# Attention backward: half of the second set of exponentials (queries on the partitions) taken by DMA transposes of the stored score tiles, the other half still recomputed

## The chip, the cores and the metric

One core of one Trainium2 chip. Times are device microseconds of one execution. Every kernel was run several times beside runs of the kernel before on the same chip. Ratios are the mean time of one kernel's fast runs over that of the other's in the same rounds, so they are not quite the ratio of the medians that are quoted beside them.

## The reference

A gated sum of attention without a mask (32 heads of 18, sequence 2048, width 576) and a state-space convolution, with the gradients of all inputs. The change touches only attention, forward and backward. What matters of it:

```python
qkv = (x @ wqkv).reshape(B, S, 3, H, Dh).transpose(2, 0, 3, 1, 4)
scores = jnp.einsum("bhqd,bhkd->bhqk", q, k) * (Dh ** -0.5)
p = softmax(scores, axis=-1)
o = jnp.einsum("bhqk,bhkd->bhqd", p, v)
# the backward pass (jax.vjp) needs, per head:
#   dP = dO V^T,  dS = P * (dP - rowsum(dO * O)),  dQ = dS K,  dK = dS^T Q,  dV = P^T dO
```

## The kernel before

Four heads form a group (8 groups), 512 queries a query block (4 per group). A group and a query block form a unit: 32 units. A unit is walked in 32 half steps, one key tile of 128 for two of the four heads in each; eight half steps are called a round here. In each half step the kernel starts the forward pass of one unit and the backward pass of the unit before it:

- P1: scores with keys on the partitions; their exponentials `PT` are kept (20 tiles of 4 KB per partition).
- P2: `dP` with keys on the partitions; VectorE multiplies it by the kept `PT` and gives `ds`. A DMA transpose makes `dsT` (queries on the partitions) of each finished `ds`.
- P3: the scores again, now with queries on the partitions; their exponentials `eb` feed dV, which contracts over queries.

```python
def row(kind, g, b, l, r, j):                      # one score matmul: 19 rows, one of four row groups
    tg, nb = ("dP", 2) if kind == "P2" else ("S", 4)
    ps = apsp.tile([P, KB], F32, tag=tg, bufs=nb, name="ps_" + kind)
    mm(ps, lhsT=l[r0:r0 + DA], rhs=r[r0:r0 + DA], tile_position=(r0, 0))
...                                                # cut: bursts dv, dq, dk; eight or sixteen matmuls
                                                   # into the one bank accB, then one VectorE addition
for G in range(NTOT + OFF + 16):                   # half steps; the backward pass runs OFF = 37 later
    ...                                            # cut: rows P1 P3 P2 P1 P3 P2
    if G % 4 == 1 and G2 >= 4:  evs.append(dv_burst(...))
    if G % 4 == 2 and G2 >= 5:  evs.append(dq_burst(...))
    if G % 4 in (3, 0) and G2 >= 10: ...           # dK: half a burst, seven and eight half steps
                                                   # after the last ds that it needs
    if G % 4 in (3, 0) and G >= 3: ...             # PV (exponentials times V) of the forward pass, into accO
    for (kind, g, b, i, j, ps) in rows:
        if kind == "P1":
            nc.scalar.activation(U["PT"][i][:, j, :], ps, ACT.Exp)
        elif kind == "P3":
            nc.scalar.activation(e, ps, ACT.Exp)   # e = U["eb"][...]
        else:
            nc.vector.tensor_tensor(U["ds"][i][:, j, :], ps, U["PT"][i][:, j, :], op=A.mult)
            if U["dsn", i] == 4:
                nc.sync.dma_start_transpose(out=U["dsT", p][:, i % 2, :, :], in_=U["ds"][i]...)
```

The kernel shares out eight PSUM banks: four for scores (`S`), two for `dP`, one for `accO`, one for `accB`. All DMAs are issued by SyncE into one queue, in order. The order of TensorE, ScalarE, VectorE and GpSimd is the source's; SyncE's is chosen by the scheduler of the language.

## Time and profile before

| | before |
|---|---|
| median of the first three runs | 4017.24 us (4016.9 to 4019.89) |
| attention, first score matmul to last use of `dsT` | 247.6 to 2587 us |
| both passes running, 290 to 2580 us: PE, ACT, DVE busy | 98%, 91%, 80% |
| DMA share and rate there | 0.79, 139 GB/s |
| one unit, from its first dP matmul to the next unit's: second, third, last, first query block of a group | 70.4, 70.4, 76.8, 71.3 us |

The last row is worked out from the start times of the dP matmuls in the trace. Units of the second and third query block are called middle units below; those of the last and first one lie around a change of group, where the gradients of a group are stored and the next group's operands come in. A middle unit of 70.4 us is four rounds of 17.6 us. The lines behind the other rows stand in the prediction.

### The profile page before, as it was taken

Reading aid. Unit: us, or ns where it says so; the run is one execution under the profiler, and the core shown is the slowest. Engines: PE = TensorE matmul, PEld = TensorE weight load, DVE = VectorE, ACT = ScalarE, POOL = GpSimd, SP = SyncE. Lnnn points to the kernel's source line nnn. Section 1 sums busy time; section 2 is a strip of 40 time slices with the busy share of each in tenths; the row PEclk is TensorE's granted clock in tenths of the full one; section 3 lists DMA queues with packets and bytes.
Section 4 is the critical chain, followed back from the end, with each engine's and each line's share of the span. In section 5 each row is a group of like instructions: output and inputs, shape, how many; then the busy total and the mean of one; then the engine's idle time right before and its main releaser. Section 6 shows DMA issues by size and latency. Waiting matters only on the chain. (4 is left out here: it accounts for less than half of the span.)

```text
span 4013.0 us, 64388 instructions
## 1 busy us (share of the span) xinstructions
PE 3139.8 (78%) x24050; PEld 1049.1 (26%) x24050; DVE 2959.3 (74%) x5147; ACT 2878.7 (72%) x5308; POOL 63.0 (2%) x141
## 2 busy tenths in 40 slices
PE   7979999999999999999999999779244445454411
PEld 2312222222222222222222222136133333333310
DVE  5518877878878878878878878712388888888877
ACT  4459999989989999989989989501366666666401
POOL 0000000000000000000000000100000000000000
PEclk9955555555555555555555555589555555555555
DMA  8436797886787887787887787876455565555447
GB/s 195 164 92 127 129 157 131 134 160 126 132 157 128 134 158 128 135 154 130 138 155 128 133 146 126 175 205 164 83 106 103 104 112 109 106 108 103 71 143 174
DMA packets 1858939, 538.18 MB, mean 134 GB/s; under 512 B 1771743, under 2 KB 1837353, under 8 KB 1858626
## 3 DMA queue, kind: packets, MB, share of 16 engines
q1 hardware_dynamic: 1858626, 534.07, 69.9%
q8 instruction: 189, 3.10, 0.3%
q14 instruction: 124, 1.02, 0.1%
HBM read 102.10 MB, written 60.96 MB: 41 GB/s over the span
## 5 line engine op out<-in xcount | busy, mean ns | idle before, releaser
L601 DVE TENSOR_TENSOR ds<-ps_P,PT 128x512 bf16<-128x512 f32 x2048 | 1360.8, 687 | 369.8 <-PE ps_P L30 226.0
L592 ACT ACTIVATE PT<-ps_P 128x512 bf16<-128x512 f32 x2048 | 1250.2, 615 | 186.4 <-PE ps_P L30 186.4
L596 ACT ACTIVATE eb<-ps_P 128x512 bf16<-128x512 f32 x2048 | 1262.6, 618 | 21.3 <-PE ps_P L30 21.2
L30 PE MATMUL ps_P<-dOaT,VaT_g 19*128 19x512 bf16 x2048 | 1145.0, 601 | 36.1 <-DMA VaT_g<-VaT_d 32.3
L30 PE MATMUL ps_P<-KaT_g,QaT_g 19*128 19x512 bf16 x2048 | 1105.2, 593 | 5.8 <-ACT PT L592 5.8
L30 PE MATMUL ps_P<-QaT_g,KaT_g 19*128 19x512 bf16 x2048 | 1055.0, 613 | 9.9 <-DMA KaT_g<-KaT_d 5.9
L30 PE MATMUL accO<-PT,Vtok_g 128*32 128x512 bf16 x2048 | 331.6, 632 | 0.0
L30 PEld LDWEIGHTS <-KaT_g 19*128 19x128 bf16 x2048 | 135.9, 103 | 740.9 <-issue 721.0
L30 PE MATMUL accK<-dsT,Qtok_g 128*32 128x256 bf16 x4096 | 314.8, 407 | 8.9 <-DMA Qtok_g<-QaT_d 5.7
L30 PEld LDWEIGHTS <-VaT_g 19*128 19x128 bf16 x2048 | 196.3, 98 | 383.5 <-issue 345.4
L30 PE MATMUL accQ<-ds,Ktok_g 128*32 128x512 bf16 x2048 | 266.9, 620 | 1.3 <-DVE dvacc L461 0.8
L30 PE MATMUL accV<-eb,dOa 128*32 128x512 bf16 x2048 | 267.0, 621 | 0.6 <-DVE dkacc L502 0.6
L30 PE MATMUL uvp<-RX,E1e 128*128 128x64 bf16 x1152 | 134.2, 290 | 106.1 <-DVE E1e L892 106.1
L30 PE MATMUL tps<-RX,T0w 128*128 128x32 bf16 x576 | 38.4, 233 | 215.1 <-DVE yd L1027 189.9
L873 ACT ACTIVATE kk<-ph,magc 128x512 f32<-128x512 f32 x144 | 91.1, 686 | 148.1 <-DVE E1e L891 112.7
L30 PE MATMUL ph<-thr,lrow 3*128 3x512 bf16 x288 | 127.5, 576 | 86.1 <-ACT ab L866 59.3
L30 PEld LDWEIGHTS <-QaT_g 19*128 19x128 bf16 x2048 | 158.8, 99 | 128.5 <-issue 123.0
L461 DVE TENSOR_TENSOR dvacc<-dvacc,accV 128x512 f32<-128x512 f32 x224 | 154.1, 688 | 34.4 <-PE accV L30 29.4
L478 DVE TENSOR_TENSOR dqa<-dqa,accQ 128x512 f32<-128x512 f32 x224 | 153.8, 687 | 34.0 <-PE accQ L30 28.5
L30 PEld LDWEIGHTS <-E1e 128*128 128x128 bf16 x1152 | 125.2, 124 | 127.1 <-DVE E1e L892 126.5
L30 PE MATMUL ybp<-Rw,E1n 128*128 128x31 bf16 x1152 | 70.1, 233 | 104.1 <-ACT ydi L964 101.4
L910 ACT ACTIVATE UV<-uvp 128x512 bf16<-128x512 f32 x144 | 86.0, 597 | 85.1 <-PE uvp L30 85.1
(273 smaller groups left out, 3392.2 us busy)
## 6 DMA issues: line engine op xcount, KB each, us to landing
T0w<-Kp_d SPq DMA_DIRECT2D x36, 512.0 KB
dsT<-ds SPq DMA_TRANSPOSE x512
dqkv_d<-dtk SPq DMA_DIRECT2D x96, 72.0 KB
dqkv_tok<-dqkv_d SPq DMA_DIRECT2D x1, 6912.0 KB
Md_d<-mst SPq DMA_DIRECT2D x144, 36.0 KB
ga_d<-ga_st SPq DMA_DIRECT2D x16, 288.0 KB
dxm_d<-dxm SPq DMA_DIRECT2D x16, 288.0 KB
skw<-Md_d SPq DMA_DIRECT2D x72, 64.0 KB
```

The source lines that it names most:

```text
L30: return nc.tensor.matmul(out, lhsT=lhsT, rhs=rhs, start=start, stop=stop, **kw)
L461: nc.vector.tensor_tensor(a_, a_, acc, op=A.add)
L478: nc.vector.tensor_tensor(U["dqa"], U["dqa"], acc, op=A.add)
L592: nc.scalar.activation(U["PT"][i][:, j, :], ps, ACT.Exp)
L596: nc.scalar.activation(e, ps, ACT.Exp)
L601: nc.vector.tensor_tensor(U["ds"][i][:, j, :], ps, U["PT"][i][:, j, :], op=A.mult)
L873: nc.scalar.activation(B_["kk"][h][:, 4 * q:4 * q + 4, :], ph, ACT.Identity, bias=magc, scale=1.0)
L910: nc.scalar.mul(UV[:, ri, :, c0:c0 + 8], pr, -1.0 if ri == 0 else 1.0)
```

## The change

The kernel already holds the exponentials with keys on the partitions. A transpose of such a tile gives what P3 recomputes. The change takes tiles 0 and 1 of every four this way (`PTT`), and recomputes only tiles 2 and 3. It wants to free ScalarE of a quarter of its exponentials and TensorE of a sixth of its score matmuls. To make room it rewrites the schedule of a round, takes one buffer where there were two in many places, and merges the dV part of the transposed tiles into the dK burst. Cut to its core:

```diff
-                OFF = NST + 5
+            OFF = 41
+            PTB = 22
...
+                def turn(R, k):
+                    if k == 0:
+                        U["PTT", r] = work.tile([P, 2, 4 * TPQ, P], BF, tag="PTT", bufs=1, name="PTT")
+                    nc.sync.dma_start_transpose(out=U["PTT", r][:, k, :, :], in_=U["PT"][4 * r + k].rearrange("p j q -> p (j q)"))
+
+                def q_pair(R, n_):                       # P3, for tiles 2 and 3 of four only
+                    ...
+                def dk_burst(R, k):
+                    for w in range(2 if k == 0 else 1):
+                        ...
+                                if w == 0:
+                                    l_, r_ = grp_t[g]["Qtok"][:, b * TPQ + qb, j, :], U["dsT", 2 * r + k]
+                                else:
+                                    l_, r_ = U["dOa"][:, qb, j, :], U["PTT", r]
+                        ...
+                            def fin():
+                                store_grad(a_[:, 0::2, :], g, 1, list(range(4 * r, 4 * r + 4)), 1.0)
+                                store_grad(a_[:, 1:2, :], g, 2, [4 * r, 4 * r + 1], 1.0)
...
+                    half(hs)                             # rows P1 P2 P1 P2
+                    R, c8 = divmod(hs - OFF, 8)
+                    acts = {0: "dqA pv t1", 1: "dv q0", 2: "dk2", 3: "pv", 4: "pv q1", 5: "dk4", 6: "q2 dqB t0", 7: "q3 pv"}[c8].split()
...
-                    gb = work.tile([P, KB], BF, tag="gb", name="gb")
+                    gb = work.tile([P, n, P], BF, tag="gb", bufs=1, name="gb")
```

(`dsT` from 3 buffers to 2; `gb`, `gT`, `dtk`, `dO`, `Ob`, `oT`, `dqa` from 2 to 1; `dvacc` from 4 to 2.) In the table `acts`, dk4 is the long dk burst (its last `ds` is finished in half step 3, two before), dk2 the short one, t0 and t1 ask for the two PTT transposes, a q pair (q0 to q3) is two recomputed score matmuls and their exponentials, dqA and dqB are the two dQ bursts. Half steps of a round are numbered 0 to 7, as in the prediction.

## The prediction

> **What bounds the kernel now.** I read the page first: the busy slices, then the groups. Attention runs from the first score matmul at 247.6 us to the last use of a transposed tile at 2586.9 us (the view of tile `dsT`), so it is 58% of the span, and only it is changed.
>
> ```profile
> PE   7979999999999999999999999779244445454411
> ACT  4459999989989999989989989501366666666401
> PEclk9955555555555555555555555589555555555555
> DMA  8436797886787887787887787876455565555447
> ```
>
> Each digit is a slice of 100 us. In slices 3 to 25 TensorE and ScalarE are both full, TensorE at half clock, and the DMA engines are not far behind. The window table gives the sums for the part with both passes running (columns: length, then busy time of PE, PEld, DVE, ACT, POOL with counts, granted clock, DMA share, GB/s):
>
> ```profile
> 290.00:2580.00 2290.00, 2240.32 (x16312) 522.85 (x16312) 1820.46 (x2997) 2084.74 (x4145) 39.50 (x92) 0.50 0.79 139
> ```
>
> PE 98%, ACT 91%, DVE 80%, DMA 0.79. The list of waits in the attention stretch says which of the two full engines leads:
>
> ```profile
> DVE ds L601 <- PE ps_P L30: 204.8, 356, 2.9
> ACT PT L592 <- PE ps_P L30: 168.2, 412, 5.4
> ...
> PE ps_P L30 <- ACT PT L592: 5.0, 20, 0.3
> ```
>
> ScalarE and VectorE wait for TensorE; TensorE waits 5 us in all for ScalarE. **TensorE's queue is the bound**, with ScalarE just under it. The timeline gives its beat:
>
> ```profile
> 1502.12 0.60 PE L30 MATMUL ps_P<-QaT_g,KaT_g 19*128 19x512 bf16 x1
> ...
> 1502.52 0.63 PE L30 MATMUL ps_P<-QaT_g,KaT_g 19*128 19x512 bf16 x1
> ...
> 1503.10 1.04 PE L30 MATMUL accQ<-ds,Ktok_g 128*32 128x512 bf16 x8
> 1504.08 0.60 PE L30 MATMUL ps_P<-QaT_g,KaT_g 19*128 19x512 bf16 x1
> ```
>
> Score matmuls on different row groups start together, so they go in waves: six per half step in two or three waves, 0.40 us apart, and 0.53 us from the last wave to a burst. A burst of eight 512-column matmuls takes 0.98 us. Half steps alternate between 1.96 us and 2.30 us (1502.12, 1504.08, 1506.38, 1508.34), so eight of them, which I call a round, take 4 x 4.26 = 17.0 us. There are 1024 half steps, 128 rounds, 32 units (a group and a query block) of 4 rounds. 128 x 17.0 = 2181 us; the other 109 us of the 2290 are the fp32 transposes after each forward pass and the stalls where a group changes.
>
> **What the Trainium skill says.** "TensorE: Matmul & The Clock Gate", Part 1, knows two states of the clock, half and full, and gives 426.7 ns start to start for 512 columns at half; the trace agrees (0.50 for the whole stretch, waves 0.39 to 0.45 us apart). It has granted half already with TensorE 98% busy, so I expect no better from a kernel that keeps TensorE less busy. "ScalarE: Activation LUTs", What ACT_TABLE_LOAD costs, gives 186 ns + 0.833 ns per element and an overlap of about 93 ns, that is 613 ns long and 520 ns apart for 512; the trace has 0.60 to 0.62 us and a closer 0.48 us apart. "Advanced Engine Details and Errata", X-Bar Transpose (TRN2), says that transpose DMAs are as fast as regular ones, and "DMA: Bandwidth & Descriptors", Latency and other measured facts, has 261 GB/s for one with a non-contiguous middle dimension. Here both are too high for the transpose in question:
>
> ```profile
> 1563.00:1563.50 0.50, 0.50 (x11) 0.14 (x8) 0.50 (x2) 0.50 (x2) 0.00 (x0) 0.50 0.76 152
> 1563.50:1564.00 0.50, 0.50 (x8) 0.00 (x0) 0.50 (x2) 0.50 (x2) 0.00 (x0) 0.50 1.13 214
> 1564.00:1564.50 0.50, 0.50 (x8) 0.23 (x5) 0.47 (x2) 0.50 (x2) 0.00 (x0) 0.50 1.16 212
> 1564.50:1565.00 0.50, 0.50 (x6) 0.10 (x1) 0.50 (x2) 0.50 (x2) 0.00 (x0) 0.50 1.17 218
> 1565.00:1565.50 0.50, 0.50 (x7) 0.14 (x8) 0.46 (x2) 0.50 (x2) 0.00 (x0) 0.50 1.14 209
> 1565.50:1566.00 0.50, 0.50 (x8) 0.00 (x0) 0.50 (x1) 0.50 (x2) 0.00 (x0) 0.50 0.23 44
> 1566.00:1566.50 0.50, 0.50 (x7) 0.13 (x5) 0.21 (x2) 0.50 (x2) 0.00 (x0) 0.50 0.00 0
> ```
>
> One `dsT` transpose of 512 KB (524,288 bytes) fills all 16 engines for about 2.6 us with ramps, at 209 to 218 GB/s; the straight loads before attention reach over 400 GB/s. Back to back I take 524 KB / 214 = 2.45 us. A share above 1 means that packets overlap: this is the engines' own limit for this form, not a gap to be filled.
>
> **The change on TensorE, ScalarE and VectorE.** Per round: 16 recomputed score matmuls become 8, in four pairs. The four matmuls of a half step now all lie in different row groups, so one wave. My sum, with rows 0.53 (0.40 when score matmuls follow), bursts 0.85 or 0.98 where the mode changes, a PV 0.43 or 0.56, a q pair 0.40, the long dk burst 1.84: 1.94 + 1.94 + 1.51 + 1.09 + 1.52 + 2.37 + 1.91 + 1.49 = **13.8 us**, against 17.0. The columns of the bursts stay equal: half of the dV work only moves from `eb` to `PTT`. ScalarE goes from 32 to 24 exponentials, 15.6 to 11.7 us at 0.487. VectorE keeps 16 products at 0.607 us start to start (9.7), and its additions go from 4 x 0.69 + 2 x 0.41 to 4 x 0.69 + 0.41: about 12.9 us. If these engines were all, a round would take 14 to 14.5 us and attention would fall by about 350 us.
>
> **The change on DMA.** 512 `dsT` transposes stay and 256 `PTT` transposes of the same shape come: 6 per round instead of 4, 6 x 2.45 = **14.7 us**. The window moved 139 GB/s x 2290 us = 318 MB, 268 of it `dsT`; the other 50 MB (loads of a group at 290 to 410 GB/s, gradient transposes at 290, the 72 KB stores and loads in small pieces at about 0.6 us each) need some 240 us, 1.9 us per round. So the DMA needs 128 x (14.7 + 1.9) = 2125 us, and the old stretch was 2290. The spare 20% is spent on this.
>
> **The DMA then has to be fed without a gap, and the schedule does not allow that.** All transposes go through one queue in order, from one sequencer. A transpose starts to move 1.2 us after it is issued. I follow a round from the end of the long dk burst (fifth half step), which frees the only `PTT` buffer: the first PTT transpose moves from 1.2 to 3.65. The next `dsT` needs the products of the seventh half step: rows at 1.9, products done about 4.1, moving from 5.3 (1.65 us idle). From there four transposes run on without a gap (that `dsT`, the second PTT, two more `dsT`): 5.3 + 9.8 = 15.1. The long dk burst needs the last of them: it reads the product tile finished only two half steps earlier (before: six or seven). TensorE reaches it at 12.1 and **stalls 3 us**. It ends at 15.2 + 1.7 = 16.9. So a round is 16.9 us, what it was, before the other transfers. Of their 1.9 us some falls into the 2.2 us of gaps; most comes between the four transposes and adds to the path. I take 1.0 to 1.4: 17.9 to 18.3 us.
>
> **Sum.** 128 x 18.0 = 2304. The forward's transposes, 2 us per unit before, now mostly lie in TensorE's stall. Where a group changes it gets worse: the last unit of a group took 77 us against 70 for the others; `gb`, `gT`, `dtk`, `dO`, `Ob` and `oT` go from two buffers to one, a group's gradient stores go from 12 to 14, and dK and half of dV are stored one right behind the other, so ScalarE waits with the second `gb` until the first was transposed, behind a full queue. I put 7 to 10 us on each of 8 groups, 70. Start: four half steps more without a second pass, 5 us. 2304 + 70 + 5 = 2379 against 2290: +90, so 4017 + 90, about **4110 us**.
>
> **Rivals.** (1) The compute bound holds: if the DMA engines take PTT in their gaps and the sequencer orders issues better than the source (SyncE is not among the hand-scheduled engines), a round needs only 15.5 to 16.5 us: 4017 - 64 to 190, 3830 to 3950. For it: TensorE, ScalarE and VectorE all get room, and DMA is 21% idle. Against: it needs over 95% use of the DMA. (2) A wash: the stall takes exactly the place of the saved waves, as in my bare 16.9 us round, 3990 to 4080. (3) Single buffers and head-of-line blocking: the sequencer already waited 108 + 42 us for ScalarE before it could issue a gradient transpose, with the DMA 20% idle; now such blocking is lost DMA time. At 3 us for each of 112 stores, 4200 to 4300.
>
> **Range and chances.** 1 us per round is 128 us, and my round is no better than that. So 3960 to 4260. Faster by over 2% needs attention under 2260 us, of which some 48 have no second pass, thus 2125 of DMA in 2210, 96%: 0.13. Within 2%: 0.36. Slower by over 2%: 0.51.
>
> **What would show it.** Right: DMA share in attention up from 0.79 to 1.0 or more, about 195 GB/s; TensorE waiting for DMA `dsT` at `accK` for 150 to 400 us in all; ScalarE's busy time down by 630 us, PE's share of the stretch under 90%, ACT's under 75%; clock 0.50; exponentials in `eb` 1024; PTT transposes as long as `dsT`. Wrong: little waiting for `dsT`, or transposes back to back well under 2.45 us (then rival 1); waits mainly of ScalarE for `gT` (rival 3); or a granted clock of 1.0, which I exclude.

## The result, and the profile after

The changed kernel takes **4464.54 us** (median of 4 runs, 4458.43 to 4465.79), before 4017.07 us beside it: ratio 1.111 (95% interval 1.1091 to 1.1129), 447 us slower. The result is correct. The prediction leaned to slower; the loss was five times the 90 us forecast, outside the range.

The page's slices, as before (each digit 1/40 of the span, now 112 us):

```profile
PE   8877768767767866866776776764934544444411
ACT  5366646656656656655655665630126666666601
PEclk9855555555555555555555555556965555555555
DMA  7469989989988998999999988998645555555447
```

No engine is full any more: in most slices with both passes TensorE has fallen to six to eight tenths and ScalarE to five to six, and the DMA engines stand at eight to nine. The window over the stretch with both passes (length, PE, PEld, DVE, ACT, POOL busy, clock, DMA share, GB/s):

```profile
292.00:3027.00 2735.00, 1983.07 (x16320) 525.62 (x16318) 1726.74 (x2869) 1609.29 (x3130) 42.41 (x108) 0.55 0.92 165
```

The stretch grew from 2290 to 2735 us. TensorE is busy 257 us less in it, ScalarE 475 us less; 165 GB/s x 2735 us is 451 MB, 133 MB more than before, as 256 transposes of 524 KB should be. So the work went as intended, and waits more than replaced it. The list of waits from 300 to 3000 us (who waited for whom: total, times, longest):

```profile
ACT PT L493 <- PE ps_P L30: 731.5, 373, 5.8
PE accK L30 <- DMA dsT<-ds: 505.3, 218, 5.9
...
ACT gb L421 <- DMA gT<-gb: 182.3, 46, 8.2
PE ps_P L30 <- ACT PT L493: 173.2, 35, 9.0
...
PE ps_P L30 <- DVE ds L498: 11.3, 24, 1.0
```

ScalarE waits for TensorE, and TensorE for `dsT`. Where, the timeline of TensorE shows (start, length, instruction, idle time ahead of it and who ended it):

```profile
1718.25 0.37 PE L30 MATMUL ps_P<-dOaT,VaT_g 19*128 19x512 bf16 x1
1722.57 1.04 PE L30 MATMUL accK<-dsT,Qtok_g 128*32 128x256 bf16 x16 [3.95 <-DMA dsT<-ds]
...
1727.02 0.63 PE L30 MATMUL ps_P<-dOaT,VaT_g 19*128 19x512 bf16 x2
1729.97 1.05 PE L30 MATMUL accK<-dsT,Qtok_g 128*32 128x256 bf16 x16 [2.32 <-DMA dsT<-ds]
```

It stalls **twice** in a round, at dk2 and at dk4. Over all 128 rounds the idle time ahead of dk2 is 1.78 us in the median, 259 us in all, and ahead of dk4 2.27 us and 269 us (worked out from the trace). The 3.95 us shown at dk2 are therefore not typical: the data of its `dsT` had all moved at 1720.2, but from 1721.0 to 1722.2 the DMA moved next to nothing (5 GB/s, a 16 KB packet of the page's instruction queue starts at 1720.6), and its semaphore was complete only at 1722.5, 2.3 us after the last data; the PTT transpose before it needed 0.5 us for this. The timeline of the issuing sequencer over the same time says why dk2 waits at all:

```profile
1711.37 4.49 SPq L514 DMA_TRANSPOSE PTT<-PT  x2
1715.91 14.95 SPq L504 DMA_TRANSPOSE dsT<-ds  x4
1731.91 4.24 SPq L514 DMA_TRANSPOSE PTT<-PT  x2
```

In the source a `dsT` stands between t0 and t1. In the queue the two PTT transposes are neighbours (in 121 of the 128 rounds), and the `dsT` that dk2 needs lies behind both. At dk4 it is something else: that `dsT` was issued at 1725.53 with the DMA engines idle, and the burst waited for its bare latency, 4.4 us from issue to burst. The sequencer's line, and windows of the DMA (last two columns: share, GB/s):

```profile
1725.53 1.94 SPq L504 DMA_TRANSPOSE dsT<-ds  x1
```

```profile
1723.80:1726.70 2.90, 2.90 (x20) 0.51 (x18) 2.70 (x5) 2.17 (x4) 0.00 (x0) 0.50 0.00 0
1726.70:1729.30 2.60, 0.95 (x6) 0.04 (x6) 1.45 (x3) 2.04 (x4) 0.00 (x0) 0.50 1.05 202
```

For 2.9 us nothing moved: TensorE's stall at dk2 had held back the products, and there was nothing to issue. Then one transpose moved alone while TensorE stood at dk4. In such a round the two take turns: TensorE waits for the DMA, and then the DMA for TensorE.

From the start times of the dP matmuls, as before (median per half step in middle units; the sum of the medians is called an undisturbed round, and it lies below the mean round: 17.3 against 17.6 us before the change, 19.4 against 19.7 after it):

| half step | 0 | 1 | 2 | 3 | 4 | 5 | 6 | 7 | round |
|---|---|---|---|---|---|---|---|---|---|
| predicted TensorE work | 1.94 | 1.94 | 1.51 | 1.09 | 1.52 | 2.37 | 1.91 | 1.49 | 13.8 |
| changed kernel | 2.10 | 1.92 | 3.32 | 1.41 | 2.06 | 4.74 | 1.95 | 1.87 | 19.4 |
| `e1`: PTT without its volume | 2.11 | 1.92 | 2.11 | 1.42 | 2.06 | 4.77 | 1.95 | 1.87 | 18.2 |

Units by query block (second, third, last, first): 77.8, 80.1, 93.1, 92.1 us, against 70.4, 70.4, 76.8, 71.3. If all units had grown by the 8.6 us of the middle ones, 32 x 8.6 = 274 us would be lost; the units around a change of group grew by another 8 to 12 us each, some 160 us over 16 units.

### The profile page after: what moved, and what is told of

Same layout as the page of the kernel before. It is cut to its first block, busy times and chain, and to the rows that moved or that the text cites. A ratio compares the mean times of both kernels' runs of the same rounds, so it can differ in the third digit from the quotient of the medians.

```text
span 4464.0 us, 63571 instructions
## 1 busy us (share of the span) xinstructions
PE 2890.1 (65%) x24050; PEld 1055.1 (24%) x24050; DVE 2865.8 (64%) x5019; ACT 2405.4 (54%) x4300; POOL 65.7 (1%) x157
## 5 line engine op out<-in xcount | busy, mean ns | idle before, releaser
L493 ACT ACTIVATE PT<-ps_P 128x512 bf16<-128x512 f32 x2048 | 1120.3, 612 | 734.0 <-PE ps_P L30 733.1
L30 PE MATMUL ps_P<-dOaT,VaT_g 19*128 19x512 bf16 x2048 | 756.9, 572 | 44.1 <-DMA VaT_g<-VaT_d 30.1
L30 PE MATMUL ps_P<-QaT_g,KaT_g 19*128 19x512 bf16 x2048 | 696.4, 575 | 134.7 <-ACT PT L493 128.6
L535 ACT ACTIVATE eb<-ps_P 128x512 bf16<-128x512 f32 x1024 | 561.3, 610 | 177.2 <-PE ps_P L30 175.8
L30 PE MATMUL ps_P<-KaT_g,QaT_g 19*128 19x512 bf16 x1024 | 351.0, 584 | 49.4 <-ACT PT L493 46.5
L459 DVE TENSOR_TENSOR dkacc<-dkacc,accK 128x512 f32<-128x512 f32 x192 | 106.2, 553 | 413.9 <-PE accK L30 413.9
L30 PEld LDWEIGHTS <-Qtok_g 128*32 128x32 bf16 x4096 | 125.7, 125 | 722.6 <-issue 480.2
L918 DVE SCALAR_TENSOR_TENSOR kk<-kk,ph 128x512 f32<-128x512 f32 x144 | 95.1, 682 | 71.2 <-ACT kk L913 71.2
L30 PEld LDWEIGHTS <-Vtok_g 128*32 128x32 bf16 x2048 | 61.5, 110 | 331.8 <-issue 329.4
L30 PE MATMUL accK<-PTT,dOa 128*32 128x256 bf16 x2048 | 138.7, 420 | 0.0
```

The source lines that it names most:

```text
L30: return nc.tensor.matmul(out, lhsT=lhsT, rhs=rhs, start=start, stop=stop, **kw)
L459: nc.vector.tensor_tensor(a_, a_, acc, op=A.add)
L918: nc.vector.scalar_tensor_tensor(v_, v_, MAGIC, B_["ph"].pop((h, q)), op0=A.subtract, op1=A.subtract)
```

## The experiments

All times are medians of 4 runs, beside runs of the kernel before (4017 to 4026 us). Units are given as second, third, last and first query block.

| run | time, us | ratio to before (95%) | units, us |
|---|---|---|---|
| changed kernel | 4464.5 | 1.111 (1.1091 to 1.1129) | 77.8, 80.1, 93.1, 92.1 |
| e1_small_ptt (wrong) | 4272.9 | 1.062 (1.0600 to 1.0642) | 72.7, 74.1, 86.9, 85.3 |
| e2_late_dk | 4230.7 | 1.051 (1.0495 to 1.0530) | 70.7, 70.2, 87.9, 84.6 |
| e3_two_store_buffers | 4403.8 | 1.095 (1.0925 to 1.0967) | 77.6, 80.2, 92.8, 84.7 |
| e4_before_more_dma | 4138.1 | 1.028 (1.0267 to 1.0298) | 70.4, 72.1, 85.6, 75.7 |
| e5_late_small (wrong) | 4138.0 | 1.029 (1.0269 to 1.0315) | 70.4, 70.4, 82.2, 79.7 |
| e6_late_two_store | 4161.6 | 1.035 (1.0324 to 1.0369) | 69.6, 71.2, 83.7, 79.6 |
| e7_small_two_store (wrong) | 4222.0 | 1.050 (1.0472 to 1.0520) | 73.0, 74.3, 83.8, 81.3 |
| e8_before_one_store | 4043.7 | 1.005 (1.0021 to 1.0081) | 70.4, 70.4, 76.5, 73.6 |
| e9_late_small_dp3 (wrong) | 4173.0 | 1.039 (1.0367 to 1.0404) | 70.8, 70.4, 84.8, 79.9 |
| e10_late_two_store_dp3 | 4152.7 | 1.033 (1.0303 to 1.0354) | 68.9, 69.7, 83.8, 79.3 |
| e11_late_small_accb2 (wrong) | 4211.9 | 1.048 (1.0451 to 1.0501) | 72.0, 71.9, 85.8, 81.5 |
| e12_late_two_store_even | 4158.1 | 1.033 (1.0317 to 1.0348) | 69.2, 70.8, 84.0, 79.9 |
| e13_even_spread_stores | 4154.5 | 1.032 (1.0306 to 1.0340) | 69.4, 70.6, 82.1, 81.3 |
| e14_even_spread_small (wrong) | 3973.9 | 0.989 (0.9868 to 0.9903) | 65.9, 66.9, 74.9, 74.1 |

**Take the volume of PTT away.**

```diff
-                        U["PTT", r] = work.tile([P, 2, 4 * TPQ, P], BF, tag="PTT", bufs=1, name="PTT")
-                    nc.sync.dma_start_transpose(out=U["PTT", r][:, k, :, :], in_=U["PT"][4 * r + k].rearrange("p j q -> p (j q)"))
+                        U["PTT", r] = PTT_all        # zeroed once
+                    nc.sync.dma_start_transpose(out=U["PTT", r][:, k, 0:1, :], in_=U["PT"][4 * r + k][:, 0, 0:P])
```

> The changed kernel, but each PTT transpose carries one 128x128 block of 16 (the rest of PTT stays zero, so a part of dV and its products are wrong on purpose). All instructions, their order and their waits stay; only the DMA time of PTT, 256 x 2.6 us, goes. Theory A (TensorE waits for score-gradient transposes that lie in the queue behind two PTT transposes): the wait of TensorE for dsT at accK falls from 516 us to 50 to 250 us (the dk burst of the fifth half step still follows its product by two half steps), middle units from 78-80 us to 64-70 us, total 3950 to 4130 us. Theory B (the bursts come too soon after their products, however full the queue is): the wait stays over 350 us, total over 4300 us. Theory C (single store buffers): units at the change of a group stay over 90 us, total over 4250 us.

Measured: 4272.9 us, between the theories. In the table of half steps only number 2 moved, from 3.32 to 2.11 us: the stall at dk2 is the queue's doing. Half step 5 stayed at 4.77 us: the stall at dk4 does not come from the volume of PTT. By bursts, the idle time ahead of dk2 fell from 259 to 73 us, ahead of dk4 only from 269 to 264 us. Of the wait for `dsT`, 516 us over the whole trace of the changed kernel, more than half was left (window 292 to 2960 us):

```profile
PE accK L30 <- DMA dsT<-ds: 328.0, 165, 4.4
```

So A and B each hold for one of the two stalls, and more than half of the loss (447 us, of which 192 went here) is not volume. No run put only the order of the queue right, so how much of the stall at dk2 comes from the order, and how much from the volume in whatever order, is not separated.

**Let the bursts run later.** dk4 from half step 5 to the next round's 0, dk2 from 2 to 4, the PTT requests to 1 and 2.

```diff
-  {0: "dqA pv t1", 1: "dv q0", 2: "dk2", 3: "pv", 4: "pv q1", 5: "dk4", 6: "q2 dqB t0", 7: "q3 pv"}
+  {0: "pv dk4", 1: "dv q0 t0", 2: "dqA t1", 3: "pv", 4: "pv dk2", 5: "q1 q2", 6: "dqB", 7: "q3 pv"}
-  PTB = 22   ... tag="eb", bufs=12
+  PTB = 23   ... tag="eb", bufs=8
```

> The changed kernel with the same transposes, but each dk burst runs five half steps after the last product that it needs, instead of two or three, and the PTT transposes are asked for in half steps 1 and 2; right results. Theory A/B (exposed latency in the chain product, queue, transpose, burst): TensorE's wait for dsT falls under 200 us, middle units to 68-73 us (near the DMA's own 6 x 2.6 us per round and what else it moves), total 4100 to 4250 us. If the DMA engines' capacity alone is the limit (they were moving something 86% of the time), at most 14% of the 2735 us can go: total not under 4080 us. If neither is right, it stays within 40 us of 4464 us.

Measured: 4230.7 us. The wait for `dsT` is gone (2.6 us are left in the list), and middle units are back at 70.5 us, what they were before the change. Theory A/B is confirmed for the middle units, with whole transposes and the PTT pairs still neighbours in most rounds. Those around a change of group stayed at 85 to 88 us, 14 to 17 above the middle.

**Give the stores their second buffer back.** `gb`, `gT`, `dtk`: `bufs=1` to `bufs=2`; `eb` 12 to 9.

> The changed kernel with two buffers each for gb, gT and dtk (as before the change), paid for with three fewer buffers of eb. Theory C (ScalarE waits 182 us for gb to be transposed, at the ends of groups, and everything behind it): the two units around the change of a group fall from 93 us by 5 to 10 us each, total 4464 - 80 to 160 us. Theory A (the queue is the limit there too, and ScalarE's wait only shows it): total falls by under 40 us.

Measured: 4403.8 us, 61 us less. ScalarE's wait for `gb` fell from 182 to 43 us, but only the unit of the first query block became shorter (92.1 to 84.7); that of the last one kept its 92.8 us. Between the two forecasts: the buffers cost something, not the whole.

**The same transposes in the kernel before.** 256 transposes of `PT` tiles into a buffer that nobody reads, in half steps 1 and 5; `eb` 12 to 10, `oT` 2 to 1.

```diff
+                    X = work.tile([P, 4 * TPQ, P], BF, tag="XT", bufs=1, name="XT")
+                    nc.sync.dma_start_transpose(out=X, in_=UN[(g, b)]["PT"][4 * (R % 4) + k].rearrange("p j q -> p (j q)"))
```

> The kernel before with 256 more transposes of its stored score tiles into a buffer that nobody reads; all else stays, but for one buffer less of oT and two less of eb. It has six to seven half steps between a product and its dk burst. DMA need: 768 x 2.6 us and some 300 us of other transfers, about 2300 us against an attention of 2337 us. Theory A/B (the short distance in the changed schedule is what hurts): 4017 to 4120 us. If the volume of the transposes alone explains the loss: over 4300 us.

Measured: 4138.1 us, 113 us more than before, a little outside the first forecast. The second query block's unit stayed at 70.4 us and the third's grew by 1.7: with seven and eight half steps between product and burst (the recorded texts count one less), half as many transposes again are hidden almost completely. The cost lies around a change of group (85.6 and 75.7 us), where TensorE now waits for the next group's operands, 96.1 us in all instead of 32.3:

```profile
PE ps_P L30 <- DMA VaT_g<-VaT_d: 96.1, 7, 14.8
```

The window says how full the DMA engines are (share 1.07, 187 GB/s; a share over 1 means overlapping packets):

```profile
303.00:2700.00 2397.00, 2240.92 (x16300) 521.63 (x16300) 1817.49 (x2995) 2083.56 (x4141) 39.15 (x91) 0.50 1.07 187
```

**Late bursts and no volume.** The edits of e1 and e2 together.

> Late bursts (as e2_late_dk) and PTT transposes of one block in 16 (as e1_small_ptt; wrong on purpose): what the schedule costs without the DMA volume. If middle units of e2 (70.4 us) are bound by the DMA engines (24 transposes of 2.6 us and 4 to 5 us of others per unit), they fall here to 57 to 63 us. If they are bound by TensorE, VectorE or a wait between them, they stay over 68 us. Units at the change of a group: if the single store buffers set them, still 15 us or more above the middle units. Total 3800 to 3950 us in the first case, over 4130 us in the second.

Measured: 4138.0 us, and the middle units did not move: 70.4 us. That was a surprise and the most useful miss. Here TensorE waits for no transpose (2 us in all), a quarter of the exponentials and a sixth of the score matmuls are gone, and still an undisturbed round takes 17.2 us. My 13.8 us of TensorE work were wrong by more than 3 us. TensorE and VectorE around the long burst:

```profile
1614.86 0.60 PE L30 MATMUL ps_P<-dOaT,VaT_g 19*128 19x512 bf16 x1
1615.12 0.58 PE L30 MATMUL ps_P<-QaT_g,KaT_g 19*128 19x512 bf16 x1
1615.40 0.58 PE L30 MATMUL ps_P<-dOaT,VaT_g 19*128 19x512 bf16 x1
1615.91 0.62 PE L30 MATMUL accO<-PT,Vtok_g 128*32 128x512 bf16 x4
1616.31 1.07 PE L30 MATMUL accK<-dsT,Qtok_g 128*32 128x256 bf16 x16
...
1619.03 1.04 PE L30 MATMUL accV<-eb,dOa 128*32 128x512 bf16 x8 [0.25 <-DVE dkacc L459]
```

```profile
1614.07 1.28 DVE L498 TENSOR_TENSOR ds<-ps_P,PT 128x512 bf16<-128x512 f32 x2
1615.54 1.29 DVE L498 TENSOR_TENSOR ds<-ps_P,PT 128x512 bf16<-128x512 f32 x2 [0.19 <-PE ps_P L30]
1618.29 0.69 DVE L459 TENSOR_TENSOR dkacc<-dkacc,accK 128x512 f32<-128x512 f32 x1 [1.46 <-PE accK L30]
```

The four score matmuls of a half step lie in four row groups and can start at once, as they do at 1618.17 in the same trace. Here they start over half a microsecond: the second dP matmul (1615.40) starts when VectorE has done with the product banks of the half step before (1614.07 + 1.28 = 1615.35). Then the long burst runs, VectorE has nothing and idles 1.46 us, and the next burst waits for VectorE's addition out of `accB`. The waits that space out matmuls hardly show as idle time, for a matmul's record is 0.6 us long and covers them; they show in the distance of the starts.

**Late bursts with two store buffers.** Offset 39, 22 score tiles, `gb`, `gT`, `dtk` double.

> Late bursts as in e2_late_dk and two buffers of gb, gT and dtk as in e3; the room is found by an offset of 39 half steps and 22 score tiles. Right results. In e2 ScalarE waited 232 us for gb and the units at the change of a group took 85 and 88 us against 70.4. If the single buffers are what remains, these units fall to 75 to 80 us and the total to 4050 to 4130 us. If the DMA queue is full there anyhow, they stay over 82 us and the total over 4160 us.

Measured: 4161.6 us; the units around a change of group 83.7 and 79.6 us, which is neither forecast clearly. ScalarE's wait for `gb` fell from 232 to 82 us, but TensorE's wait for the next group's `VaT` rose to 63 us: what a buffer gives is partly taken by the queue.

**No volume, two store buffers, bursts as changed.** The edits of e1 and e3.

> PTT transposes of one block in 16 (wrong on purpose) and two store buffers, dk bursts where the change put them: what is left is the short distance between product and burst alone. Middle units as in e1, 72 to 75 us. Units at the change of a group: in e1 85 and 87 us; with two buffers 76 to 81 us if the buffers set them. Total 4130 to 4200 us.

Measured: 4222.0 us, middle units 73 to 74.3 as expected; around a change of group 83.8 and 81.3, a little above the forecast. Without volume and with the buffers such a unit is still 9 us longer than a middle one.

**One store buffer in the kernel before.**

> The kernel before with one buffer each of gb, gT and dtk instead of two, nothing else. There its stores come at different half steps and never two behind each other. If single buffers cost by themselves, the two units at the change of a group lengthen by 5 us or more and the total by 40 to 120 us. If it takes the pairwise stores and the fuller queue of the changed kernel, it stays within 25 us of before.

Measured: 4043.7 us, 24 us by the medians and half a per cent, at the edge of the second forecast. The single buffers are cheap here, where stores do not follow each other and the queue is not full; which of the two makes them cheap is not separated.

**Share out PSUM differently.** e9: scores 4 banks to 3, products 2 to 3, on e5. e10: the same on e6. e11: scores 3, products 2, `accB` 2, on e5.

```diff
-                    tg, nb = ("dP", 2) if kind == "P2" else ("S", 4)
+                    tg, nb = ("dP", 3) if kind == "P2" else ("S", 3)
```

> As e5_late_small (late bursts, PTT transposes of one block in 16, wrong on purpose), but PSUM is shared out as three banks for scores and three for products dP instead of four and two. In e5 there was hardly a wait for DMA left, and a round still took 17.1 us where my sum of TensorE work was 13.8 us. Theory D (TensorE and VectorE take turns because only two product banks exist: VectorE idles while a long burst runs and TensorE waits for VectorE after it): a round falls to 15.0 to 16.2 us, middle units from 70.4 to 61 to 66 us, total 3850 to 4020 us. Rival (TensorE's own work is 17 us and my sum was wrong; or three score banks are too few for ScalarE): middle units stay over 68 us.

> As e6_late_two_store (right results, whole PTT transposes), with three banks for scores and three for products. If theory D holds, the DMA engines become the bound in the middle units: 24 transposes of 2.6 us and some 4 us of others, 65 to 68 us against 69.6 to 71.2 in e6; total 4050 to 4120 us. If D does not hold, within 40 us of e6 (4162 us).

> As e5_late_small, with three banks for scores, two for products and two for the burst sums accB. If what TensorE loses is the wait of the next burst for VectorE's addition out of the single accB bank (0.3 us twice a round in the timeline of e5), middle units fall by 2 to 4 us from 70.4. If the product banks are the cause, by less than 1.5 us.

Measured: 4173.0, 4152.7 and 4211.9 us: nothing gained, and theory D's forecast failed. By half steps, e9 against e5: number 0 fell from 3.31 to 2.80 us and number 3 from 1.79 to 1.09, as D says; but 5 rose from 2.27 to 2.76 and 7 from 1.52 to 2.35, half steps with recomputed scores: TensorE now waits 37 us in all for the exponentials into `eb` to free a score bank, a wait that e5's list does not have. The third product bank shortened the half steps that D names, so the turn-taking is real; in the three ways tried of sharing eight banks it only moved. e11 shortened half steps 0 and 1 (2.80 and 1.78 us), left 3 as it was, and did the same harm in 5 and 7.

**Spread the acts evenly.** On e6: each q pair beside a PV, the long burst alone.

```diff
-  {0: "pv dk4", 1: "dv q0 t0", 2: "dqA t1", 3: "pv", 4: "pv dk2", 5: "q1 q2", 6: "dqB", 7: "q3 pv"}
+  {0: "dk4", 1: "dv q0 t0", 2: "dqA t1", 3: "pv q1", 4: "pv dk2", 5: "pv q2", 6: "dqB", 7: "q3 pv"}
```

> As e6_late_two_store, with the acts of a round spread evenly: one q pair beside each PV (half steps 1, 3, 5, 7), the long dk burst alone in its half step, PV in half steps 3, 4, 5, 7. My sum of the longer of TensorE and VectorE per half step is 14.8 us. If e6's round of 17.1 us came from uneven half steps (3.3 us in one, 1.5 us in the next, with only two product banks between the engines), a round falls to the DMA engines' 15.8 to 16.8 us: middle units 65 to 68 us, total 4010 to 4090 us. If not, middle units stay over 69 us and the total over 4130 us.

Measured: 4158.1 us, no gain in time over e6 and far above the 4010 to 4090 us forecast, but a change in kind. The sum of the median half steps fell from 17.1 to 15.9 us: an undisturbed round is now shorter than before the change (17.3). Yet the mean round is 17.5 us. The windows show the whole stretch, and 20 us in the middle of it:

```profile
292.00:2700.00 2408.00, 2030.16 (x16245) 549.49 (x16244) 1720.15 (x2859) 1616.01 (x3127) 40.63 (x104) 0.52 1.05 186
1640.00:1660.00 20.00, 18.81 (x146) 5.01 (x138) 16.40 (x31) 15.07 (x30) 0.00 (x0) 0.50 1.17 204
```

By the packets' times the DMA engines were moving something in 96% of 320 to 2650 us, in runs of up to 55 us without a gap, the four longest at 195 to 200 GB/s. The DMA is now the bound, as e14 below confirms by taking volume away.

**Part the paired stores.** On e12, the second store of a pair three half steps later.

> As e12, with the second of the two gradient stores after a dk burst put three half steps later instead of right behind the first. If the pairs of stores are what makes the units at the change of a group long (79.6 and 83.7 us in e6), these fall by 3 to 6 us each, the total by 50 to 100 us below e12, and ScalarE's wait for gb under 40 us. If the full DMA queue sets them, within 25 us of e12.

Measured: 4154.5 us, the same as e12. Where the queue is full, moving the stores does not help.

**Take the volume out of that.**

> As e13_even_spread_stores, with PTT transposes of one block in 16 (wrong on purpose). In e12 and e13 the DMA engines were busy in 96% of the time and moved 186 GB/s, and undisturbed rounds took 15.4 to 15.9 us, yet the mean round was 17.5 us. If the DMA volume is now the only bound, taking away 256 x 2.6 us of it brings middle units from 70 to 62 to 65 us and those at the change of a group from 82 to 66 to 74 us, total 3850 to 3970 us, below the kernel before. If TensorE and VectorE or the stores hold it, middle units stay over 68 us, total over 4060 us.

Measured: **3973.9 us**, 1.15% below the kernel before, with middle units of 66 us (a little above the forecast of 62 to 65) and 74 to 75 us around a change of group. It computes a wrong dV, so it is no version to use; it says what the change would bring if its transposes were free. Its DMA window:

```profile
292.00:2520.00 2228.00, 2016.25 (x16219) 544.21 (x16222) 1717.07 (x2851) 1612.80 (x3122) 41.17 (x104) 0.52 0.83 145
```

No correct version beat the kernel before.

## Why the prediction was right or wrong

The chain changed kernel, e13, e14, before takes the loss apart: 1.111 - 1.032 = 0.079, about **316 us, is the schedule and its buffers** (e13 moves the same bytes); 1.0323 - 0.9885 = 0.044, about **176 us, is the volume** of the transposes under the best schedule found; and 0.9885 - 1 = -0.0115, **46 us, is what the saved engine work is worth in that schedule**, with its waits around a change of group. The sum is 446 us, as measured. Another chain would share it out differently: the same volume was worth 196 us in the changed kernel (e1), 181 with two store buffers (e3 to e7), but only 89 with late, uneven bursts (e2 to e5).

- *TensorE is the bound before, at half clock.* Right as far as tested: e4 put half as many transposes again on the DMA and middle units stayed at 70.4 and 72.1 us.
- *The transposes go at 2.45 us each back to back, 2125 us in all.* Too low. Full queues moved 186 to 204 GB/s with everything in them: 451 MB at 200 GB/s are 2260 us, and e12 needed 2408 us. By this estimate there was next to nothing to gain in a stage that took 2290 us before. That 209 to 218 GB/s are "the engines' own limit for this form" is not so either: from 1722.4 to 1723.6 in the changed kernel the rest of a `dsT`, alone in the queue after the pause, moved at 290 GB/s. What holds a steady queue of transposes to less was not tested.
- *If the engines were all, attention would fall by 350 us.* This step was off by most. e14, with nearly free transposes, gained 44 us. The sum added up TensorE's waves and bursts, 13.8 us, and VectorE's work, 12.9, and put the round just above the longer of the two, as if the one could run ahead of the other. With two product banks and one `accB` they take turns: an undisturbed round was 17.2 us in e5 and 15.9 us when evenly spread. It did not make the forecast wrong by itself, as I let the DMA's chain set the round.
- *One stall of 3 us at the long dk burst, so a bare round of 16.9 us, and 17.9 to 18.3 with the other transfers.* This is the step that made the forecast wrong: a round of one stall, behind four transposes that run on without a gap. The runs showed two stalls, 259 us at dk2 and 269 us at dk4, and DMA gaps between them. The stall at dk4 was there and nearly as large (4.74 us in the half step against 2.37 of work, 2.4 us), but not for the reason given: no chain of four transposes ended there, as the DMA was all but idle when its `dsT` was issued (under 20 GB/s in the 1.1 us around the issue in 83 of 128 rounds), and with PTT's volume gone (e1) the stall stayed. That its size came near was luck. The stall at dk2 had no place in the forecast: I had the second PTT transpose behind the seventh half step's `dsT`, as in the source. In the queue it lay ahead of it, so dk2 stalled as well: 3.32 us in the half step against 1.51. With 0.2 to 0.6 us more in half steps 0, 3, 4 and 7 (0.16 + 0.32 + 0.54 + 0.38 = 1.4 us, which I put down to the turn-taking) a bare round became 19.4 us. Mean middle units of 79 us are 19.7 us per round, against the 18.0 us in the forecast: 128 x 1.7 = 220 us of the 356 us by which the stretch was longer than forecast.
- *70 us around the changes of group.* Mis-sized. These 16 units cost 92.6 us, 13.6 more than the middle ones, 218 us where I put 70 on top of the rounds (before, 74.0 against 70.4, 58 us). e3 puts 61 us of it on the single store buffers, e4 shows that the volume alone lengthens the last unit of a group by 9 us; the two overlap. What is left when both are mended is still 8 us over a middle unit in e14, and that I have not settled.
- *The granted clock stays at half.* Wrong in part: 0.55 in the mean, see below. A faster clock cannot be what made the kernel slower.
- *The signs.* DMA share 0.92 at 165 GB/s instead of 1.0 at 195: TensorE's stalls left gaps that I did not expect. TensorE's wait for `dsT` 505 us instead of 150 to 400. PE 73% and ACT 59% of the stretch: right. ScalarE's busy time fell by 473 us and not by 630: that figure counts 1024 exponentials at their full 0.615 us, while at the prediction's own 0.487 us from start to start it is 499. The remaining 26 us I put down to exponentials that now stand alone and do not overlap a neighbour.
- *The rivals.* Rival 1, the compute bound at 15.5 to 16.5 us, did not come: even e14, with nearly free transposes, took 15.9 us for an undisturbed round, 16.6 in the mean. Rival 3, the blocked queue with single buffers, came nearest (4200 to 4300; its own 3 us for each of 112 stores on 4017 would be 4353) and named one of the causes, yet 4464.5 us lies well above it: the larger loss was two stalls in each of 128 rounds.

## What to carry to other kernels

Before work is moved to a DMA queue, ask how many half steps lie between a transfer's source being ready and its first use: here seven and eight hid nearly all of 256 extra transposes in the middle units (e4), five hid them too (e2), and two to three exposed the existing ones as well, though no instruction was slow. When an engine's own work is summed for a forecast, look for the buffers between it and its neighbour: with two or one of them neither can run ahead, and here a round whose longer side was 13.8 us took 17.2 us with uneven steps and 15.9 with even ones. And read the order of the queue from the compiled program: the scheduler may put a transfer that is not urgent ahead of one that is.

## What the Trainium skill lacked or had wrong

- "Advanced Engine Details and Errata", X-Bar Transpose (TRN2), and "DMA: Bandwidth & Descriptors", Latency and other measured facts: the first calls transposes as fast as regular DMAs, the second has 261 GB/s for one with a non-contiguous middle dimension. A transpose of 512 KB from SBUF to SBUF moved at 209 to 218 GB/s here, the straight loads before attention at over 400, and a full queue of transposes with small transfers between them at 186 to 204 GB/s. Behind a pause the rest of one moved at 290 GB/s for 1.2 us (1722.4 to 1723.6 in the changed kernel).
- "DMA: Bandwidth & Descriptors", Latency and other measured facts, has about 600 ns to the first byte of a hardware-generated DMA. For a transpose into an idle queue it was 1.2 us from the start of the issue (1725.53 to 1726.7), and the data took 2.6 us more.
- "TensorE: Matmul & The Clock Gate", Part 1, says that a busy TensorE is granted the full clock. Here the kernel before kept TensorE 98% busy for 2290 us and was granted 0.50 throughout, while the changed kernel, 73% busy, was granted 0.55 in the mean, with stretches at full clock (columns as above; the clock is the third number from the right):

```profile
1713.00:1714.00 1.00, 0.90 (x9) 0.28 (x6) 1.00 (x3) 1.00 (x3) 0.00 (x0) 1.00 1.15 215
```

- "ScalarE: Activation LUTs", What ACT_TABLE_LOAD costs: it has an overlap of about 93 ns. In the kernel before, neighbouring exponentials of 512 columns started 0.48 us apart (1501.42 and 1501.90, the first 0.60 us long), an overlap of 0.12 us.
- No page that I read says that a wait of a score matmul for a PSUM bank can leave no idle time in the trace, because the record of the matmul before, on another row group, covers it; here the starts in e5 (1614.86, 1615.12, 1615.40, each record about 0.6 us long) were the only sign.
